# The first phase of a gated-scan and expert kernel: constants and small products to GpSimd, its products in halves, other step and store times

## The chip, the cores and the metric

One core of one Trainium2 chip runs the whole program. The metric is device time in microseconds (us) for one execution; lower is better. TensorE (PE) does matrix products and transposes, VectorE (DVE), ScalarE (ACT) and GpSimd (POOL) do elementwise work, and SyncE (SP) only issues transfers (DMA). Each engine runs its own instruction list in order. GpSimd also issues transfers, those whose rows are picked by a list of indices.

## What is computed

Two steps follow each other. First a gated recurrence runs along 4 sequences of 5056 positions with 256 features. Then each of the 20224 resulting rows is given to one of 8 experts, at most 2528 rows each, by going through all row-expert scores from the largest down; every expert is a two-layer network.

```python
f = lower_bound + (1 - lower_bound) * sigmoid(f_logit)
for t in range(S):
    h = f[:, t] * h + (1 - f[:, t]) * x[:, t]
    y[:, t] = h
...
logits = x @ w_gate
for idx in np.argsort(-logits.flatten()):
    tok, e = idx // E, idx % E
    if assigned[tok] >= 0 or counts[e] >= cap:
        continue
    assigned[tok] = e
...
out[mask] = np.maximum(x[mask] @ w1[e], 0) @ w2[e]
```

## The kernel before

The program has two phases. This document is about the first one, which I call the prelude: it takes about the first 159 us.

**The prelude's loop.** The rows are cut into 158 tiles of 128, and the loop `for i in range(NCH + 1)` takes them in 40 chunks of four tiles (the last has two). In pass `i`, SP issues the load of chunk `i+3` (`load`: one transfer for the gate logits, into tile `fl`, one for x, into tile `xl`; four buffers of each). `fwd(i)` transposes both on TensorE (into PSUM tiles `pf` and `pb`), ScalarE makes the gate `f` (tile `fg`) from `pf`, and VectorE runs the recurrence as two scans into tile `g`. `sig(i+2)` takes the sigmoid of a later chunk on ScalarE and then multiplies it into x on GpSimd, one instruction of 1024 columns. `back(i-1)` multiplies the scanned chunk by a matrix `iw` that turns it back and gives the 8 router scores (PSUM tile `pr`); VectorE and ScalarE copy `pr` into the row tile `hr`, GpSimd copies the scores into `X`, and SP stores `hr` to the scratch array `hbuf` in DRAM. There are 22 buffers for `hr`, so stores can lag; `SR = 0.5` and the line with `stored` say how far.

**What runs beside it.** `build(2)` emits two deferred VectorE instructions per pass that make constants. `prep(c0, c1)` finds the best expert of 32 tiles at a time, in five steps: a maximum (`M`), a comparison (`TMP`), a product with `kc` (on GpSimd up to tile 128, except the last piece before tile 72), another maximum (`A`), and a one-hot table (`O`). `early` picks one expert from the first 72 tiles, loads its weights by index (tile `r`), lists 896 of its rows (`g1` is a comparison of a ramp `IO` with an offset; `blocks` makes the row numbers `ids`), and `first_rows` gathers these rows from `hbuf`. `early` yields once per pass; each resumed piece goes to the head of a pass, ahead of `fwd(i)`'s scans on VectorE.

**The second phase** (`moe`) starts with transposes of the gathered rows (tile `pt`) and runs the experts while the rest of the assignment is worked out beside them. `Pace` keeps a count of expected engine times, by which small pieces of work are placed between matrix products; the order is fixed when the program is built.

In the profile nearly all instructions carry the line of one helper, L100, so they are told apart by the tiles that they write and read.

Of the kernel before, what the change touches and what calls it, by code (L numbers as in the profile page):

```python
# [106 lines left out]
def kernel(ctx: ExitStack, tc: tile.TileContext, x: bass.AP, f_logit: bass.AP,  # L107
# [9 lines left out]
    P = 128  # L117
# [27 lines left out]
    chunks = [(t0, min(KT, NT - t0), min(KT, NT - t0) * P // KT) for t0 in range(0, NT, KT)]  # L145
    NCH = len(chunks)
    RING = 22
    SR = 0.5
    PS, RW, CP = 2, NT - CE, 136
    LA = 4  # L150
    SPIN = (9, 4), (5, 2)

# [57 lines left out]
    late = []  # L210

    class Later:
        def __getattr__(self, op):
            return lambda *args, **kw: late.append((op, args, kw))
    lv = Later()

    def build(n):
        while late and n:
            op, args, kw = late.pop(0)
            getattr(nc.vector, op)(*args, **kw)  # L220
            n -= 1
    kc = consts.tile([P, E], F32, name="kc")
    lv.tensor_scalar(kc, IO[:, :E], -1.0, float(E), op0=OP.mult, op1=OP.add)


    IO8 = IO[:, :16].unsqueeze(2).to_broadcast([P, 16, 8])
    njt = []
    for st in (256.0, 16.0, 1.0):
        t = consts.tile([P, 16, 8], F32, name=f"njt{int(st)}")
        lv.tensor_scalar(t, IO8, st, None, op0=OP.mult)  # L230
        njt.append(t)
    thr0 = consts.tile([P, 16, 8], I16, name="thr0")
    lv.tensor_scalar(thr0, IO8, 4096.0, -32768.0, op0=OP.mult, op1=OP.add)
    tri = consts.tile([P, P], BF, name="tri")
    lv.tensor_scalar(tri, IO[:, :P], pv, None, op0=OP.is_gt)
    ones = consts.tile([P, P], F32, name="ones")
    lv.memset(ones, 1.0)
    onec = consts.tile([P, NX], F32, name="onec")
    lv.memset(onec, 1.0)
# [6 lines left out]
    lv.tensor_copy(fi, ii)  # L246
    bm = consts.tile([P, 8, E], F32, name="bm")
    lv.tensor_scalar(bm, IO[:, :8].unsqueeze(2).to_broadcast([P, 8, E]), fi[:, 1:2], None,
                            op0=OP.is_equal)

    selv = consts.tile([P, 16], F32, name="selv")
    lv.tensor_scalar(selv, IO[:, :16], fi[:, 2:3], None, op0=OP.is_equal)
# [8 lines left out]
    lv.tensor_scalar(j16, IO[:, :16].unsqueeze(2).to_broadcast([P, 16, E]), 1.0, None, op0=OP.add)  # L261

    at16 = consts.tile([P, 16, E], F32, name="at16")
    lv.tensor_copy(at16, IO[:, :16].unsqueeze(2).to_broadcast([P, 16, E]))
    lv.memset(at16[:, 0], 16.0)

    nsub = consts.tile([P, P], BF, name="nsub")
    prev = consts.tile([P, P], F32, name="prev")
    lv.tensor_scalar(prev, IO[:, :P], -1.0, pv, op0=OP.add, op1=OP.is_equal)
    lv.tensor_tensor(nsub, ident, prev, op=OP.subtract)  # L270
# [18 lines left out]
    wb = consts.tile([P, 3], F32, name="wb")  # L289
    wk = consts.tile([P, 3], F32, name="wk")  # L290
    for j, (m, o) in enumerate(((2 * P, 0), (2 * P, P), (P, 0))):
        lv.tensor_scalar(wb[:, j:j + 1], pv, float(E * m + o), None, op0=OP.add)
        lv.memset(wk[:, j:j + 1], float(-m))


    X = state.tile([P, NC, E], F32, name="X")
# [431 lines left out]
    def early(wi, ids):  # L728

        def sums(ps):  # L730
            for g in range(CE // 8):
                nc.tensor.matmul(ps[:, :64], ones_b, O[:, 8 * g:8 * g + 8].rearrange("p c e -> p (c e)"), start=(g == 0),
                                 stop=(g == CE // 8 - 1))
        yield sums
        ps = beside[0]
        v.tensor_reduce(SC8, ps[:, :64].rearrange("p (c e) -> p e c", e=E), AX.X, OP.add)
        v.tensor_scalar(Q8, SC8, float(EARLY), 1.0e6, op0=OP.is_lt, op1=OP.mult)
        v.tensor_tensor(Q8, Q8, SC8, op=OP.add)
        v.tensor_reduce(few, Q8, AX.X, OP.min)
        yield  # L740
        v.scalar_tensor_tensor(Q8, Q8, few, kc, op0=OP.is_equal, op1=OP.mult)
        v.tensor_reduce(ecode, Q8, AX.X, OP.max)
        v.scalar_tensor_tensor(wi, wk, ecode, wb, op0=OP.mult, op1=OP.add)
        first_weights(0)
        yield
        ranks(0, CE)
        first_weights(1)
        yield
        first_weights(2)
        w = CE + 2  # L750

# [12 lines left out]
        g1 = {}  # L764
        nb = EARLY // P
        for b0 in range(0, nb, 2):
            n = min(2, nb - b0)
            if b0 % 4 == 0:
                g1 = ohp.tile([P, 512], BF, name="g1")
                v.tensor_scalar(g1, IO, st[:, b0 // 4:b0 // 4 + 1], None, op0=OP.is_ge)  # L770
                yield

            def rows(ps):
                for b in range(n):
                    nc.tensor.matmul(ps[:, b * w:(b + 1) * w], g1[:, (b0 + b) % 4 * P:((b0 + b) % 4 + 1) * P],
                                     RAE[:, :w], start=(b == 0), stop=(b == n - 1), skip_group_check=True)
# [66 lines left out]
    def sig(i, which=None, between=lambda: None):  # L843
        np_ = chunks[i][2]
        if which is not False:
            for a, b in halves(0, i):
                nc.scalar.activation(FT[i][:np_, a:b], FT[i][:np_, a:b], AF.Sigmoid, scale=-1.0)
        if which is not True:
            for a, b in halves(1, i):
                mine = 1 < i < NCH - 1  # L850
                (nc.gpsimd if mine else nc.vector).tensor_mul(XT[i][:np_, a:b], FT[i][:np_, a:b], XT[i][:np_, a:b])
                if a == 0:
                    between()

# [11 lines left out]
    def fwd(i):  # L866
# [29 lines left out]
    def back(i, job=None):  # L896
        t0, n, _ = chunks[i]
        HR[i] = pring.tile([P, KT, ROW], F32, name="hr")
        for k in range(n):
# [43 lines left out]
    def prep_step(n):
        while preps and n:
            at = next(preps[0], None)
            if at is None:
                preps.pop(0)
            else:
                n = n - 1 if at == 'k' else 0
# [32 lines left out]
    for i in range(NCH + 1):  # L982
# [736 lines left out]
```

## Time and profile before

| what | value |
|---|---|
| median of three runs | 1148.47 us (1148.03 to 1148.62) |
| the profiled execution: time | 1148.47 us |
| its span, first to last instruction | 1146.7 us |
| TensorE busy over the span | 1129.9 us (99%) |
| TensorE busy in 100 to 150 us | 48.41 of 50 |
| TensorE busy in 250 to 300 us | 50.00 of 50 |
| first transpose of the second phase starts | 158.69 us |

The span lies 1.77 us below the time of the same execution. Times in the rows below count from the span's start. A row of a timeline gives the start, the duration, the engine, the operation with its tiles, and in square brackets how long the engine sat idle before it and what ended that. Neighbouring instructions of one kind are merged into a row with their count.

### The profile page before, as it was taken

What the parts mean: (1) busy time and instruction counts of PE and PEld (TensorE: products, weight loads), DVE (VectorE), ACT (ScalarE), POOL (GpSimd) and SP (SyncE); (2) the same over time, 40 slices, a digit from 0 to 9 for tenths busy, and PEclk for the clock granted to TensorE, in tenths of its full rate; (3) what the DMA queues carried; (4) which work ended last, traced back from release to release, by engine and by line L of the source; (5) the groups of instructions that cost most, each with busy time, mean ns of one, the idle gap of its engine ahead of it and who ended that gap; (6) DMA issues with size and microseconds to landing.
All of it is one profiled execution on the core that took longest, in us unless ns stands there. A gap on an engine that the chain in (4) does not pass through costs nothing.

```text
span 1146.7 us, 21286 instructions
## 1 busy us (share of the span) xinstructions
PE 1129.9 (99%) x7905; PEld 1008.9 (88%) x7905; DVE 764.8 (67%) x2233; ACT 542.1 (47%) x1141; POOL 477.6 (42%) x486
## 2 busy tenths in 40 slices
PE   9999989999999999999999999999999999999997
PEld 7999879989888888888889888898889888888887
DVE  7999997778777446776875877656444643463342
ACT  7889873263337532643544444345434532242221
POOL 5777642243335663333433433343334333433322
PEclk9999999999999999999999999999999999999999
DMA  9999995131131111311311311131113111321100
GB/s 353 374 355 371 394 341 152 38 112 43 48 111 39 40 52 50 115 48 42 120 47 43 112 47 41 48 115 48 46 43 110 58 42 49 108 62 46 42 32 32
DMA packets 52947, 125.23 MB, mean 109 GB/s; under 512 B 8563, under 2 KB 28789, under 8 KB 51685
## 3 DMA queue, kind: packets, MB, share of 16 engines
q0 software_dynamic: 20016, 61.01, 16.5%
q1 hardware_dynamic: 32544, 62.78, 15.5%
q8 instruction: 64, 1.05, 0.4%
q14 instruction: 47, 0.38, 0.1%
q10 hardware_dynamic: 276, 0.01, 0.0%
HBM read 81.79 MB, written 42.10 MB: 108 GB/s over the span
## 4 chain that ended last, share of the span: by engine, by line
PE 91%; DMA 3%; DVE 2%; issue 1%; ACT 1%; POOL 1%; POOLq 0%; DVEq 0%; ACTq 0%; SPq 0%
PE pw L100 39%; PE py L100 35%; PE rt L100 7%; PE pr L100 5%; PE pb L100 2%; PE pf L100 2%; DVE g L100 1%; PE pt L100 1%; DMA fl<-in_f_logit_dram 1%; DMA hbuf<-hr 1%; DMA r<-in_moe_w_dram,wi 1%; DVE hl L100 0%; ACT fg L100 0%; POOL out_dram L100 0%; ACT hh L100 0%
## 5 line engine op out<-in xcount | busy, mean ns | idle before, releaser
L100 PE MATMUL py<-w2s,hh 128*128 128x256 f32 (+2 forms) x2120 | 434.4, 296 | 0.0
L100 ACT ACTIVATE hh<-pw 128x512 fp32r<-128x512 f32 (+3 forms) x328 | 190.8, 582 | 496.9 <-PE pw L100 439.7
L100 DVE SCALAR_TENSOR_TENSOR hl<-pw,hh 128x512 fp32r<-128x512 f32 (+3 forms) x328 | 219.3, 669 | 214.4 <-ACT hh L100 213.1
L100 PEld LDWEIGHTS py<-w2s,hh 128*128 128x128 f32 (+1 forms) x2120 | 341.9, 188 | 20.8 <-issue 0.2
L100 PE MATMUL py<-w2s,hl 128*128 128x256 f32 x1136 | 319.8, 282 | 0.0
L100 POOL DMA_INDIRECT out_dram<-y,ids x160 | 162.7, 1017 | 304.7 <-ACT hh L100 248.2
L100 POOL DMA_INDIRECT fl<-hbuf,ids x160 | 164.4, 1028 | 267.6 <-ACT hh L100 193.6
L100 PE MATMUL pw<-xh,xl 128*128 128x512 f32 (+3 forms) x672 | 231.6, 387 | 1.2 <-DVE hl L100 0.9
L100 PEld LDWEIGHTS py<-w2s,hl 128*128 128x128 f32 x1136 | 212.8, 187 | 2.0
L100 PEld LDWEIGHTS pw<-xh,xl 128*128 128x128 f32 x672 | 124.8, 189 | 19.5 <-DVE hl L100 1.3
L100 PE MATMUL pw<-xl 128*128 128x512 f32 (+3 forms) x336 | 130.5, 389 | 0.1
L100 PE MATMUL pw<-xl,w1h 128*128 128x512 f32 (+1 forms) x320 | 127.0, 397 | 0.0
L100 PE MATMUL pw<-xh,w1h 128*128 128x512 f32 (+1 forms) x320 | 126.3, 395 | 0.0
L100 PE MATMUL pw<-xh,w1l 128*128 128x512 f32 (+1 forms) x320 | 126.2, 394 | 0.0
L100 POOL TENSOR_TENSOR xl<-fl,xl 128x1024 f32<-128x1024 f32 x37 | 87.7, 2369 | 40.2 <-ACT fl L100 22.0
L100 DVE TENSOR_TENSOR_SCAN g<-fg,g,pb 128x512 f32<-128x512 f32 (+4 forms) x78 | 92.8, 1227 | 6.8 <-ACT fg L100 6.1
L100 PE MATMUL pr<-iw,g 128*128 128x136 f32 x632 | 81.1, 280 | 0.5 <-ACT hr L100 0.5
L100 ACT ACTIVATE junk<-rt,r 128x182 bf16<-128x182 f32 (+2 forms) x153 | 61.4, 402 | 37.3 <-DVE r L100 32.7
L100 PEld LDWEIGHTS pr<-iw,g 128*128 128x128 f32 x632 | 76.4, 190 | 1.0 <-ACT hr L100 0.9
L100 PEld LDWEIGHTS pw<-xh,w1l 128*128 128x128 f32 x320 | 60.2, 188 | 11.3
L100 PEld LDWEIGHTS pw<-xl 128*128 128x128 f32 x336 | 63.7, 190 | 5.9 <-DVE xl L100 0.5
L100 PEld LDWEIGHTS pw<-xh,w1h 128*128 128x128 f32 x320 | 60.4, 189 | 8.0
(271 smaller groups left out, 1537.6 us busy)
## 6 DMA issues: line engine op xcount, KB each, us to landing
hbuf<-hr SPq DMA_DIRECT2D x39, 528.0 KB, 9.9
fl<-in_f_logit_dram SPq DMA_DIRECT2D x38, 512.0 KB, 6.7
xl<-in_x_dram SPq DMA_DIRECT2D x38, 512.0 KB, 7.2
fl<-hbuf,ids POOLq DMA_INDIRECT x160, 2.8
out_dram<-y,ids POOLq DMA_INDIRECT x160, 2.4
fl<-in_f_logit_dram SPq DMA_DIRECT2D x3, 256.0 KB, 4.1
xl<-in_x_dram SPq DMA_DIRECT2D x3, 256.0 KB, 4.5
r<-in_moe_w_dram,wi POOLq DMA_INDIRECT x27, 5.3
```

Source lines behind the costliest of these rows:

```text
L100: r = f(*args, **kw)
```

## The change

Eight edits, all in the prelude. Constants that VectorE made are made on GpSimd, partly ahead of the loop. The GpSimd product of each chunk is cut into two instructions of 512 columns (for chunk 2 the second half goes to VectorE). In `prep` the product with `kc` goes to GpSimd for all pieces up to tile 136, and two passes lie between it and the maximum that reads it; each pass runs one step. In `early` four small operations go to GpSimd and two of its steps come a pass later each. The comparison `g1` is written in the form that also adds up its result (into a column that nobody reads). `f` is made by a copy with a constant 1.0 instead of an identity with a column of ones. The third `hr` copy of even chunks below 18 goes from VectorE to ScalarE. Stores run at 0.6 of the passes up to the 18th, then pause, then go on one per pass from pass 35.

```diff
-    SR = 0.5
-    PS, RW, CP = 2, NT - CE, 136
+    SR = 0.6
+    RW, CP = NT - CE, 136
...
     kc = consts.tile([P, E], F32, name="kc")
-    lv.tensor_scalar(kc, IO[:, :E], -1.0, float(E), op0=OP.mult, op1=OP.add)
+    ramp(kc, [[-1, E]], E)
...
-    lv.tensor_scalar(tri, IO[:, :P], pv, None, op0=OP.is_gt)
+    lg_.tensor_scalar(tri, IO[:, :P], pv, None, op0=OP.is_gt)
...
-        v.tensor_scalar(Q8, SC8, float(EARLY), 1.0e6, op0=OP.is_lt, op1=OP.mult)
-        v.tensor_tensor(Q8, Q8, SC8, op=OP.add)
+        nc.gpsimd.tensor_scalar(Q8, SC8, float(EARLY), 1.0e6, op0=OP.is_lt, op1=OP.mult)
+        nc.gpsimd.tensor_tensor(Q8, Q8, SC8, op=OP.add)
+        yield
         v.tensor_reduce(few, Q8, AX.X, OP.min)
+        nc.gpsimd.tensor_scalar(Q8, Q8, few, None, op0=OP.is_equal)
+        nc.gpsimd.tensor_tensor(Q8, Q8, kc, op=OP.mult)
         yield
-        v.scalar_tensor_tensor(Q8, Q8, few, kc, op0=OP.is_equal, op1=OP.mult)
         v.tensor_reduce(ecode, Q8, AX.X, OP.max)
...
-                v.tensor_scalar(g1, IO, st[:, b0 // 4:b0 // 4 + 1], None, op0=OP.is_ge)
+                v.tensor_scalar(g1, IO, st[:, b0 // 4:b0 // 4 + 1], 0.0, op0=OP.is_ge, op1=OP.add, accum_out=esc[:, 6:7])
...
                 mine = 1 < i < NCH - 1
-                (nc.gpsimd if mine else nc.vector).tensor_mul(XT[i][:np_, a:b], FT[i][:np_, a:b], XT[i][:np_, a:b])
+                for c, e in ((a, (a + b) // 2), ((a + b) // 2, b)) if mine else ((a, b),):
+                    (nc.gpsimd if mine and (i > 2 or c == 0) else nc.vector).tensor_mul(XT[i][:np_, c:e], FT[i][:np_, c:e], XT[i][:np_, c:e])
...
-            nc.scalar.activation(f[:, h, :w], pf[h][:, :w], AF.Identity, scale=nomlb[:, h:h + 1], bias=one)
+            nc.scalar.activation(f[:, h, :w], pf[h][:, :w], AF.Copy, scale=nomlb[:, h:h + 1], bias=1.0)
...
-            if k == 0 or k == 2 and i % 2 == 0 and i < CE // KT:
+            if k == 0:
                 nc.vector.tensor_copy(HR[i][:, k], pr)
...
-        few_ = c1 == CE
-        far = nc.gpsimd if c1 <= 128 and not few_ else v
         v.tensor_reduce(m_, x_, AX.X, OP.max)
-        yield 'end' if few_ else 'k'
         v.tensor_tensor(t_, x_, bcl(m_, e - c0), op=OP.is_ge)
-        yield 'k'
-        far.tensor_tensor(t_, t_, bce(kc, e - c0), op=OP.mult)
-        yield 'k'
+        (nc.gpsimd if c1 <= CP else v).tensor_tensor(t_, t_, bce(kc, e - c0), op=OP.mult)
+        yield
+        yield
         v.tensor_reduce(a_, t_, AX.X, OP.max)
-        yield 'end' if few_ else 'k'
+        if not CE - 8 <= c1 <= CE:
+            yield
         v.tensor_tensor(O[:, c0:e], bce(kc, e - c0), bcl(a_, e - c0), op=OP.is_equal)
-        yield 'k'
+        yield
...
-        if i + 2 < NCH:
-            sig(i + 2)
+        for k in range(i + 2 - (i == 1), min(i + 3, NCH) if i else 0):
+            sig(k)
...
-            while stored < min(i - 1, int(SR * (i - 1)) + (i > 30)):
+            while stored < min(i - 1, max(min(int(SR * i), CE // KT), CE // KT + i - NCH + 6)):
                 store(TURN[stored])
                 stored += 1
-        if i >= 4:
-            build(2)
+        if i >= 2:
+            build(4)
...
-        prep_step(99 if i == NCH else 3 if done == CE and upto < CE + 8 else PS if done < CE else (i != NCH - 4) + (i > NCH - 3))
+        prep_step()
```

The first place is VectorE's list at the first `prep` piece (passes 9 to 12). A scan is printed there as SCALAR_TENSOR_TENSOR `g<-fg,g,pb`, two per pass. Before:

```order
L100 TENSOR_REDUCE M_171<-X 128x32
L100 TENSOR_TENSOR TMP<-X,M_171 128x256
L100 SCALAR_TENSOR_TENSOR g<-fg,g,pb 128x512 x2
L100 COPY hr<-pr 128x264
L100 TENSOR_SCALAR bm<-IO,fi 128x64
L100 TENSOR_SCALAR selv<-IO,fi 128x16
L100 TENSOR_REDUCE A_172<-TMP 128x32
L100 SCALAR_TENSOR_TENSOR g<-fg,g,pb 128x512 x2
```

The same place in the changed kernel:

```order
L100 TENSOR_REDUCE M_186<-X 128x32
L100 TENSOR_TENSOR TMP<-X,M_186 128x256
L100 SCALAR_TENSOR_TENSOR g<-fg,g,pb 128x512 x2
L100 COPY hr<-pr 128x264
L100 SCALAR_TENSOR_TENSOR g<-fg,g,pb 128x512 x2
L100 COPY hr<-pr 128x264
L100 TENSOR_REDUCE A_187<-TMP 128x32
L100 SCALAR_TENSOR_TENSOR g<-fg,g,pb 128x512 x2
```

The maximum `A`, which reads GpSimd's product, stood one pair of scans behind the comparison `TMP`, and now stands two pairs behind it; the constants `bm` and `selv` are gone from VectorE here.

The second place is VectorE's list at the second `g1` of `early`. Before, it stood alone between two pairs of scans, in pass 34:

```order
L100 COPY hr<-pr 128x264
L100 TENSOR_SCALAR g_2081<-IO,st 128x512
L100 SCALAR_TENSOR_TENSOR g<-fg,g,pb 128x512 x2
L100 COPY hr<-pr 128x264
```

In the changed kernel it comes in pass 36, in its summing form, behind the two first steps of the last `prep` piece:

```order
L100 COPY hr<-pr 128x264
L100 TENSOR_REDUCE M_186<-X 128x32
L100 TENSOR_TENSOR TMP<-X,M_186 128x256
L100 TENSOR_SCALAR g_2223,esc<-IO,st 128x512
L100 SCALAR_TENSOR_TENSOR g<-fg,g,pb 128x512 x2
```

Three instructions now share the place that one had.

The third place is SP's list at the end of the loads, up to the last one (64 rows). Before:

```order
L923 DMA hbuf<-hr 128x4x264 x2
L181 DMA fl<-in_f_logit_dram 128x1024
L181 DMA xl<-in_x_dram 128x1024
L181 DMA fl<-in_f_logit_dram 128x1024
L181 DMA xl<-in_x_dram 128x1024
L923 DMA hbuf<-hr 128x4x264
L181 DMA fl<-in_f_logit_dram 128x1024
L181 DMA xl<-in_x_dram 128x1024
L181 DMA fl<-in_f_logit_dram 128x1024
L181 DMA xl<-in_x_dram 128x1024
L923 DMA hbuf<-hr 128x4x264
L181 DMA fl<-in_f_logit_dram 64x1024
```

In the changed kernel:

```order
L931 DMA hbuf<-hr 128x4x264
L181 DMA fl<-in_f_logit_dram 128x1024
L181 DMA xl<-in_x_dram 128x1024
L181 DMA fl<-in_f_logit_dram 128x1024
L181 DMA xl<-in_x_dram 128x1024
L181 DMA fl<-in_f_logit_dram 128x1024
L181 DMA xl<-in_x_dram 128x1024
L181 DMA fl<-in_f_logit_dram 128x1024
L181 DMA xl<-in_x_dram 128x1024
L931 DMA hbuf<-hr 128x4x264
L181 DMA fl<-in_f_logit_dram 64x1024
```

Before, 18 stores stand ahead of the last load, four of them in its last stretch. Now 19 stand ahead of it, but 18 of these lie further up, and only one among the last four pairs of loads.

## Rows read from the trace of the kernel before

**Rows 1.** Chain of waits, 27 to 29 us (start, length, what).
```profile
27.00 1.85 PE pr L100 x16
28.86 0.87 PE pf L100 x8
```

**Rows 2.** Timeline, 48 to 55 us, three engines.
```profile
48.81 0.73 POOL L100 TENSOR_TENSOR TMP<-TMP,kc 128x256 f32<-128x256 f32 x1
...
49.57 0.42 DVE L100 TENSOR_REDUCE A<-TMP 128x32 f32<-128x256 f32 x1 [0.79 <-POOL TMP L100]
...
50.55 1.04 PE L100 MATMUL pf<-ident,fl 128*128 128x128 f32 x8
...
54.75 1.04 PE L100 MATMUL pf<-ident,fl 128*128 128x128 f32 x8
```

**Rows 3.** Timeline, 79 to 85 us, VectorE and TensorE.
```profile
79.16 0.42 DVE L100 TENSOR_REDUCE A<-TMP 128x32 f32<-128x256 f32 x1 [1.38 <-POOL TMP L100]
...
80.01 1.04 PE L100 MATMUL pf<-ident,fl 128*128 128x128 f32 x8
...
84.49 1.04 PE L100 MATMUL pf<-ident,fl 128*128 128x128 f32 x8
```

**Rows 4.** Timeline, 126 to 143 us, TensorE.
```profile
126.23 1.04 PE L100 MATMUL pf<-ident,fl 128*128 128x128 f32 x8
...
134.43 1.04 PE L100 MATMUL pf<-ident,fl 128*128 128x128 f32 x8
...
138.03 1.04 PE L100 MATMUL pf<-ident,fl 128*128 128x128 f32 x8
...
142.79 1.04 PE L100 MATMUL pf<-ident,fl 128*128 128x128 f32 x8
```

**Rows 5.** Timeline, 127 to 141 us, VectorE and GpSimd.
```profile
127.89 1.76 DVE L100 TENSOR_TENSOR O<-kc,A 128x256 bf16<-128x256 f32 x1
...
135.23 2.36 POOL L100 TENSOR_TENSOR xl<-fl,xl 128x1024 f32<-128x1024 f32 x1 [2.55 <-ACT hr L100]
...
135.76 2.12 DVE L100 TENSOR_SCALAR g<-IO,st 128x512 bf16<-128x512 f32 x1
...
137.54 0.41 POOL L100 COPY X<-hr 128x32 f32<-128x32 f32 x1
137.80 2.44 DVE L100 TENSOR_TENSOR_SCAN g<-fg,g,pb 128x512 f32<-128x512 f32 x2
...
140.16 0.40 DVE L100 COPY hr<-pr 128x264 f32<-128x264 f32 x1
```

**Rows 6.** Timeline, 103 to 105 us, GpSimd and VectorE.
```profile
103.09 2.38 POOL L100 TENSOR_TENSOR xl<-fl,xl 128x1024 f32<-128x1024 f32 x1
...
104.20 0.28 DVE L100 TENSOR_SCALAR_CACHE_REDUCE EM<-A,esc 128x72 f32<-128x72 f32 x1
```

**Rows 7.** Timeline, 117 to 123 us; then transfers in 112 to 142 us.
```profile
117.73 1.04 PE L100 MATMUL pf<-ident,fl 128*128 128x128 f32 x8
...
118.77 1.06 ACT L100 ACTIVATE fl<-fl 128x1024 f32<-128x1024 f32 x1 [2.56 <-DMA fl<-in_f_logit_dram]
...
122.27 1.04 PE L100 MATMUL pf<-ident,fl 128*128 128x128 f32 x8
...
DMA packets 4838, 11.89 MB, mean 396 GB/s; under 512 B 353, under 2 KB 2667, under 8 KB 4707
```

**Rows 8.** Timeline, 147 to 161 us: the gathers and the second phase's first transposes.
```profile
147.22 1.08 POOL L100 DMA_INDIRECT fl<-hbuf,ids  x1 [2.77 <-DMA hbuf<-hr]
...
158.69 0.38 PE L100 MATMUL pt<-identr,fl 128*128 128x128 f32 x2
160.09 0.28 PE L100 MATMUL pt<-identr,fl 128*128 128x128 f32 x1 [1.03 <-DMA fl<-hbuf,ids]
```

**Rows 9.** Window 160 to 170 us: busy time of PE, PEld, DVE, ACT, POOL; granted clock; DMA.
```profile
160.00:170.00 10.00, 8.38 (x30) 5.92 (x31) 8.50 (x16) 6.98 (x11) 0.77 (x3) 0.83 1.09 350
```

**Rows 10.** ScalarE groups, shapes kept apart, 20 to 150 us: busy, mean ns, idle before.
```profile
L100 ACT ACTIVATE fg<-pf,one,nomlb 128x512 f32<-128x512 f32 x68 | 49.3, 781 | 1.5
```

More of the change, by code (lines that the diff above doesn't have):

```diff
@@ L212, with __init__, ramp @@
     class Later:
+        def __init__(self, eng):
+            self.eng = eng
         def __getattr__(self, op):
-            return lambda *args, **kw: late.append((op, args, kw))
-    lv = Later()
+            return lambda *args, **kw: late.append((self.eng, op, args, kw))
+    lv, lg_ = Later(nc.vector), Later(nc.gpsimd)
     def build(n):
         while late and n:
-            op, args, kw = late.pop(0)
-            getattr(nc.vector, op)(*args, **kw)
+            eng, op, args, kw = late.pop(0)
+            getattr(eng, op)(*args, **kw)
             n -= 1
+    def ramp(t, pattern, base=0, channel=0):
+        nc.gpsimd.iota(t, pattern=pattern, base=base, channel_multiplier=channel, allow_small_or_imprecise_dtypes=True)
     kc = consts.tile([P, E], F32, name="kc")
-    lv.tensor_scalar(kc, IO[:, :E], -1.0, float(E), op0=OP.mult, op1=OP.add)
-    IO8 = IO[:, :16].unsqueeze(2).to_broadcast([P, 16, 8])
+    ramp(kc, [[-1, E]], E)
     njt = []
-    for st in (256.0, 16.0, 1.0):
-        t = consts.tile([P, 16, 8], F32, name=f"njt{int(st)}")
-        lv.tensor_scalar(t, IO8, st, None, op0=OP.mult)
+    for st in (256, 16, 1):
+        t = consts.tile([P, 16, 8], F32, name=f"njt{st}")
+        ramp(t, [[st, 16], [0, 8]])
         njt.append(t)
     thr0 = consts.tile([P, 16, 8], I16, name="thr0")
-    lv.tensor_scalar(thr0, IO8, 4096.0, -32768.0, op0=OP.mult, op1=OP.add)
     tri = consts.tile([P, P], BF, name="tri")
-    lv.tensor_scalar(tri, IO[:, :P], pv, None, op0=OP.is_gt)
+    lg_.tensor_scalar(tri, IO[:, :P], pv, None, op0=OP.is_gt)
     ones = consts.tile([P, P], F32, name="ones")
-    lv.memset(ones, 1.0)
+    nc.gpsimd.memset(ones, 1.0)
     onec = consts.tile([P, NX], F32, name="onec")
-    lv.memset(onec, 1.0)
+    nc.gpsimd.memset(onec, 1.0)
+    lg_.tensor_scalar(thr0, njt[0], 16.0, -32768.0, op0=OP.mult, op1=OP.add)
     ii = consts.tile([P, 3], I32, name="ii")
@@ L245 @@
     fi = consts.tile([P, 3], F32, name="fi")
-    lv.tensor_copy(fi, ii)
+    lg_.tensor_copy(fi, ii)
     bm = consts.tile([P, 8, E], F32, name="bm")
-    lv.tensor_scalar(bm, IO[:, :8].unsqueeze(2).to_broadcast([P, 8, E]), fi[:, 1:2], None,
+    lg_.tensor_scalar(bm, IO[:, :8].unsqueeze(2).to_broadcast([P, 8, E]), fi[:, 1:2], None,
                             op0=OP.is_equal)
     selv = consts.tile([P, 16], F32, name="selv")
-    lv.tensor_scalar(selv, IO[:, :16], fi[:, 2:3], None, op0=OP.is_equal)
+    lg_.tensor_scalar(selv, IO[:, :16], fi[:, 2:3], None, op0=OP.is_equal)
     tot = consts.tile([P, 16, 8], F32R, name="tot")
@@ L260 @@
     j16 = consts.tile([P, 16, E], F32, name="j16")
-    lv.tensor_scalar(j16, IO[:, :16].unsqueeze(2).to_broadcast([P, 16, E]), 1.0, None, op0=OP.add)
+    ramp(j16, [[1, 16], [0, E]], 1)
     at16 = consts.tile([P, 16, E], F32, name="at16")
-    lv.tensor_copy(at16, IO[:, :16].unsqueeze(2).to_broadcast([P, 16, E]))
-    lv.memset(at16[:, 0], 16.0)
+    ramp(at16, [[1, 16], [0, E]])
+    nc.gpsimd.memset(at16[:, 0], 16.0)
     nsub = consts.tile([P, P], BF, name="nsub")
     prev = consts.tile([P, P], F32, name="prev")
-    lv.tensor_scalar(prev, IO[:, :P], -1.0, pv, op0=OP.add, op1=OP.is_equal)
-    lv.tensor_tensor(nsub, ident, prev, op=OP.subtract)
+    lg_.tensor_scalar(prev, IO[:, :P], -1.0, pv, op0=OP.add, op1=OP.is_equal)
+    lg_.tensor_tensor(nsub, ident, prev, op=OP.subtract)
     sq = consts.tile([P, 21], F32, name="sq")
@@ L291 @@
     for j, (m, o) in enumerate(((2 * P, 0), (2 * P, P), (P, 0))):
-        lv.tensor_scalar(wb[:, j:j + 1], pv, float(E * m + o), None, op0=OP.add)
-        lv.memset(wk[:, j:j + 1], float(-m))
+        ramp(wb[:, j:j + 1], [[1, 1]], E * m + o, 1)
+        nc.gpsimd.memset(wk[:, j:j + 1], float(-m))
     X = state.tile([P, NC, E], F32, name="X")
@@ L927, in prep, with prep_step @@
         x_, t_, m_, a_ = X[:, c0:e], TMP[:, c0:e], M0[:, c0:e], A1[:, c0:e]
-        few_ = c1 == CE
-        far = nc.gpsimd if c1 <= 128 and not few_ else v
         v.tensor_reduce(m_, x_, AX.X, OP.max)
-        yield 'end' if few_ else 'k'
         v.tensor_tensor(t_, x_, bcl(m_, e - c0), op=OP.is_ge)
-        yield 'k'
-        far.tensor_tensor(t_, t_, bce(kc, e - c0), op=OP.mult)
-        yield 'k'
+        (nc.gpsimd if c1 <= CP else v).tensor_tensor(t_, t_, bce(kc, e - c0), op=OP.mult)
+        yield
+        yield
         v.tensor_reduce(a_, t_, AX.X, OP.max)
-        yield 'end' if few_ else 'k'
+        if not CE - 8 <= c1 <= CE:
+            yield
         v.tensor_tensor(O[:, c0:e], bce(kc, e - c0), bcl(a_, e - c0), op=OP.is_equal)
-        yield 'k'
+        yield
     preps = []
[L943 to L949, printed above, removed]
+    def prep_step():
+        if preps and next(preps[0], preps) is preps:
+            preps.pop(0)
+            prep_step()
     sig(0, True)
@@ L1025 @@
             done += 32
[L1026 removed]
+        prep_step()
         while lows and lows[0] == 0:
```

## The prediction

> **What bounds the kernel now.** I read the busy time by stretches first: after 250 us TensorE has no idle left, so the edits can pay only in the prelude and at the step into the second phase. Then the chain of waits for the prelude. In its undisturbed stretches it is TensorE alone: a pass is the back product of 1.85 us and two groups of transposes of 0.87 us each [rows 1], together 3.6 us. I call whatever a pass takes beyond 3.6 us a stall, and read it off the starts of successive `pf` groups in the timeline of TensorE; then I look in the timelines of the other engines for what was late there. Four kinds of stall appear.
>
> First, VectorE waits for GpSimd's product `TMP`. It sits idle 0.79 us before the maximum `A` at 49.57 us, and the pass there takes 54.75 - 50.55 = 4.20 us, a stall of 0.60 [rows 2]. The same wait at 79.16 us is 1.38 us, and the pass takes 84.49 - 80.01 = 4.48 us, a stall of 0.88 [rows 3].
>
> Second, single VectorE instructions last far too long while GpSimd multiplies. A comparison `g1` lasts 2.12 us, from 135.76 to 137.88, and GpSimd's 2.36 us product runs from 135.23 to 137.59; the table `O` lasts 1.76 us [rows 5]. The scans queue behind them. The two passes from 126.23 take 8.20 us (stall 1.00), the pass from 138.03 takes 4.76 us (stall 1.16) [rows 4]. An instruction that adds up its result ran in 0.28 us in the middle of such a product [rows 6], so not every form is held.
>
> Third, ScalarE waits 2.56 us for a load at 118.77 us, shortly after the first expert's weights were fetched, and the pass takes 122.27 - 117.73 = 4.54 us (stall 0.94); from there the transfers run at 396 GB/s [rows 7].
>
> Fourth, at the step into the second phase TensorE waits 1.03 us for a gathered tile. The first gather had held GpSimd's list for 2.77 us, until a store to `hbuf` had landed [rows 8].
>
> **The change, part by part.**
>
> *Two passes between product and maximum.* The order of VectorE's list now puts two pairs of scans between the comparison and the maximum. A pair takes 2.44 us [rows 5], the product 0.73 [rows 2], so the product is there long before. Both stalls of the first kind go: 0.60 + 0.88 = 1.5 us. What would be late next there is the comparison itself, if it meets a GpSimd product (next point).
>
> *Halves and the summing form.* VectorE's room in a pass is 3.60 - 2.44 (scans) - 0.40 (`hr` copy) = 0.76 us [rows 1, 5]. A delay of the scans by up to about 0.7 us more is absorbed: the scans end 2.44 us after their `pb` group, and the second half of the next `pb` group comes 1.85 + 0.87 + 0.44 = 3.16 us after it. GpSimd's price for 512 columns comes from its two sizes, 256 columns at 0.73 us and 1024 at 2.36 [rows 2, 5]: 2.12 ns a column and 0.19 us fixed, so 1.27 us a half, 2.54 a pair. A held instruction then waits at most 1.27 us where it waited up to 2.36, provided that VectorE gets in between the halves. The rows speak for that: GpSimd's small copy that was issued at 137.54, as its product ended, lasted until 137.95, past the end of the held `g1` at 137.88, so the held instruction went ahead [rows 5]. `g1` itself, in the summing form, should not be held at all. I price it at 0.7 us: 0.28 for 72 columns [rows 6] and 0.42 for 256 in a maximum [rows 2] make 0.76 ns a column, so 0.62 for 512, and a little for the sum's own read. Below it would be 0.62, above it 2.0 (held for a half after all).
>
> What stays: in pass 31 `O` and `g1` now stand together (0.4 + 0.7; I price `O`, `M` and `TMP`, all over 256 columns, like the 0.42 of the maximum), in pass 36 `M`, `TMP` and `g1` (0.4 + 0.4 + 0.7). Free of GpSimd they overrun the room of 0.76 by 0.3 and 0.7 us, which is absorbed. With one wait for a half each they overrun by 1.6 and 2.0: stalls 0.9 and 1.3. I take the middle, 1.1 together. Of the 2.16 us of the second kind, 1.0 comes back (bounds: 2.16 and 0).
>
> [...]
>
> *ScalarE.* The gate `f` is 781 ns a half [rows 10] and now has a constant for its column of ones; the third copy of nine chunks comes to ScalarE (about 0.4 us each). Neither is on the path: in the undisturbed passes TensorE stands alone in the chain [rows 1], and where ScalarE is late it waits for a load [rows 7]. I take 0 for both. If ScalarE had no room at all, the nine copies would cost up to 3.6 us. [...]
>
> *Constants.* Some thirty small VectorE instructions go. They lay in the room of passes without a stall, except the two ahead of the wait at 49.57 us, whose time that wait hid anyway: 0. On GpSimd they and the halves must fit into 3.6 us: 2.54 + 0.2 to 0.4 for the scores' copy [rows 5] leaves over 0.6 us.
>
> *Stores.* By pass 30 there are 18 stores where there were 14, so 4 x 0.54 = 2.2 MB move ahead; then none until pass 35. Per undisturbed pass the load is 1.05 MB, and stores at 0.6 add 0.32: 1.37 MB in 3.6 us are 381 GB/s, at 0.5 they were 366. The transfers have shown 396 GB/s when backed up [rows 7], so the higher rate still fits. The weights (2.1 MB) come two passes later and again back up the queue, so I expect a wait as in rows 7 once, between passes 30 and 34. After that, with loads alone at 291 GB/s, it drains, where before it stayed full to the end. Sum 0 (bounds: 0.9 gained, 2.2 lost).
>
> *The gathers.* The last of the 18 stores that they wait for is now out by pass 30 and not 35. The wait of 2.77 us goes, the product of chunk 38 and the other gathers behind it on GpSimd move up by the same, and they have to land 1.4 us sooner against TensorE to cost nothing. 1.03 us comes back. Against it VectorE has two more small steps in this place (the last `ids`, the last `A`), some 0.3 us. I take 0.7 (bounds 0 and 1.5). [...]
>
> *Sum.* 1.5 + 1.0 + 0.7 = 3.2 us. The profiled span of 1146.7 becomes 1143.5, and with the 1.77 us around it the time is 1145.3 us; the profiled execution had the median's time, so the same holds for the median.
>
> **Rivals.**
>
> *More comes back.* Held instructions miss the products (2.1), loads no longer wait (0.9), the step gives 1.5 and a third of the clock (0.6): with 1.5 that is 6.6, 1141.9 us. For it: the pause of the stores. Against it: two places of VectorE's list got fuller.
>
> *The transfers take it back.* The earlier stores leave no slack, so every stall that goes returns as a wait for a load, and only the step pays, 0.7: 1147.8 us. For it: 396 GB/s against 381 asked. Against it: before the weights no load was late after the start, and after pass 30 the demand falls.
>
> *The halves don't do what they should*: both stand issued, and VectorE gets its turn only behind the second, so that the second kind stays at 2.16 or grows to 2.5 with the fuller places. The sum is 1.5 - 0.3 + 0.7 = 1.9: 1146.6 us. Against it stands the copy that was passed. [...]
>
> *GpSimd becomes the bound (slower).* If a half, with the waits that VectorE's own instructions put on it, takes over (3.60 - 0.25) / 2 = 1.67 us (0.25 for the scores' copy), every pass grows by the excess. From 1.8 us a half on, 0.26 us in 36 passes, 9.4 us, stand against the 3.2: 1154.7 us. From 1.72 us a half on it eats the gain (0.1 us in 36 passes), from 1.75 it is slower by more than 0.2%. Rows 2 and 5 say 1.27; against it stands only that no half of this shape has been seen.
>
> **Numbers.** A difference under 0.2% (2.3 us) can't be told from none. Forecast (gain 2.3 to 5) 0.53, more 0.13, transfers 0.14, halves 0.13, GpSimd 0.07. Faster by over 0.2%: 0.53 + 0.13 + a third of the halves = 0.70. Within: 0.14 + the rest = 0.23. Slower 0.07. The range goes from 1141.9 (the larger gain) to 1147.5, most of the way to the transfers' case; GpSimd and about a tenth beside it stay outside.
>
> **What would show it.** No wait of VectorE for `TMP`; `pf` to `pf` 3.6 us from 20 to 110 us. Halves near 1.27 us, `g1` near 0.7 wherever it falls. One late load between 118 and 130 us, none after. No wait of GpSimd for a store, and the first transpose of the second phase at 155 to 157 us instead of 158.69. I would be wrong if loads are late before 100 us, if held VectorE instructions last two halves, or if passes settle above 3.6 us with GpSimd without idle.

## The result, and the profile after

The changed kernel takes 1166.01 us (median of four runs, 1165.1 to 1167.08), the kernel before 1148.55 (1148.03 to 1149.36): a ratio of 1.0145, 95% interval 1.0133 to 1.0157. It is slower by 17.5 us, where I had forecast 3.2 us faster. The profiled execution took 1166.71 us with a span of 1164.8.

Read by stretches, the loss has one place. Windows of the changed kernel (stretch; busy us of PE, PEld, DVE, ACT, POOL with their instructions; granted clock; share of the DMA engines; GB/s):

```profile
150.00:160.00 10.00, 8.93 (x81) 8.13 (x78) 9.72 (x26) 8.43 (x17) 6.43 (x9) 1.00 1.08 357
160.00:170.00 10.00, 4.36 (x17) 2.95 (x17) 5.39 (x10) 1.93 (x2) 0.00 (x0) 0.95 1.09 343
170.00:180.00 10.00, 0.00 (x0) 0.00 (x0) 0.00 (x0) 0.00 (x0) 0.00 (x0) 0.50 0.97 302
180.00:190.00 10.00, 5.53 (x20) 4.90 (x21) 6.46 (x15) 4.24 (x8) 0.00 (x0) 0.53 0.01 4
190.00:200.00 10.00, 10.00 (x89) 8.69 (x88) 6.72 (x22) 3.23 (x10) 0.00 (x0) 1.00 0.01 2
```

For the whole of 170 to 180 us no engine computes; only the transfers run, at 302 GB/s, and TensorE's granted clock falls to 0.50; it is 0.53 in the next 10 us, and 1.00 in 190 to 200 us. Who waits for whom stands in the timeline of 158 to 190 us:

```profile
165.17 0.33 DVE L100 TENSOR_REDUCE A<-TMP 128x22 f32<-128x176 f32 x1
182.06 1.15 ACT L100 ACTIVATE w2s<-r 128x512 fp32r<-128x512 f32 x2 [20.13 <-DMA hbuf<-hr]
182.72 0.69 DVE L100 TENSOR_TENSOR w2s<-r,w2s 128x512 fp32r<-128x512 f32 x1 [17.23 <-ACT w2s L100]
183.12 0.58 ACT L100 ACTIVATE hh<-pw 128x512 fp32r<-128x512 f32 x1
...
184.47 0.80 PE L100 MATMUL pw<-xh,xl 128*128 128x512 f32 x1 [19.59 <-DVE hl L100]
...
187.20 0.63 PE L100 MATMUL py<-w2s,hh 128*128 128x256 f32 x2
```

Read it backwards. TensorE waits for `hl`, `hl` for ScalarE's `hh`, and `hh` stands behind `w2s` in ScalarE's list. `w2s` is the first expert's second weight matrix, converted from the fetched tile `r`. It waits 20.13 us, and not for its input: it waits for stores `hr` to `hbuf`. In the kernel before, the same `w2s` ran at 164.10 us with no idle before it; the first `pw` product, this `w2s` and the first `py` stand there so:

```profile
161.53 0.61 PE L100 MATMUL pw<-xh,xl 128*128 128x512 f32 x1 [0.34 <-ACT xh L100]
...
164.10 1.15 ACT L100 ACTIVATE w2s<-r 128x512 fp32r<-128x512 f32 x2
...
170.18 0.39 PE L100 MATMUL py<-w2s,hh 128*128 128x256 f32 x2
```

The changed kernel's chain of waits names the last of the stores:

```profile
173.13 8.82 DMA hbuf<-hr
```

It landed at 173.13 + 8.82 = 181.95 us, and `w2s` started at 182.06.

Why a weight tile waits for a store of rows is told by the addresses in the built program. The 22 buffers of `hr` lie from byte 115744 of SBUF on, 4224 bytes each. The second phase's pools are laid over them when the prelude's pools close. `w2s` (pool `wa2`, 16384 bytes from 149664) covers buffers 8 to 11 in both kernels, and may be written once the last rows held there are stored. Which rows these are is not fixed: a new `hr` tile takes the buffer that was released, so the order of the stores decides the order in which buffers come round. Before, buffers 8 to 11 last held chunks 18, 20, 21 and 19, which stand in the list `TURN` (the order of the stores) ahead of some 17 others. With the new rule they last held chunks 38, 39, 19 and 21, and 38 and 39 are the last stores of all.

The rows that answer to [rows 2 to 8, 10], in the changed kernel:

```profile
51.90 0.41 DVE L100 TENSOR_REDUCE A<-TMP 128x32 f32<-128x256 f32 x1
...
110.53 1.40 DVE L100 TENSOR_TENSOR TMP<-X,M 128x256 f32<-128x256 f32 x1
...
122.56 0.73 DVE L100 TENSOR_SCALAR_CACHE_REDUCE g<-IO,st 128x512 bf16<-128x512 f32 x1
...
126.26 1.06 ACT L100 ACTIVATE fl<-fl 128x1024 f32<-128x1024 f32 x1 [2.92 <-DMA fl<-in_f_logit_dram]
...
144.90 1.08 POOL L100 DMA_INDIRECT fl<-hbuf,ids  x1
...
157.96 0.54 PE L100 MATMUL pt<-identr,fl 128*128 128x128 f32 x4
...
159.19 0.49 PE L100 MATMUL pw<-xh,xl 128*128 128x512 f32 x1 [0.35 <-ACT xh L100]
```

Groups of instructions, ScalarE in 20 to 150 us and GpSimd in 10 to 158 us (busy, mean ns):

```profile
L100 ACT ACTIVATE fg<-pf,nomlb 128x512 f32<-128x512 f32 x69 | 43.7, 686 | 1.6
...
L100 POOL TENSOR_TENSOR xl<-fl,xl 128x512 f32<-128x512 f32 x73 | 92.0, 1281 | 31.3 <-ACT fl L100 21.8 <-ACT hr L100 5.6 <-PE pr L100 3.6
```

The prelude itself is faster: the wait for `TMP` is gone, the half product of GpSimd lasts 1281 ns, `g1` 0.73 us, the first gather waits for no store, and the first `pw` product starts at 159.19 us where it was 161.53. Then 2.3 us of gain meet a wait of 20 us.

### The profile page after: what moved, and what is told of

Read it like the earlier page. It is cut to its first block, busy times and chain, and to the rows that moved or that the text cites. A ratio compares the mean times of both kernels' runs of the same rounds, so it can differ in the third digit from the quotient of the medians.

```text
span 1164.8 us, 21352 instructions
## 1 busy us (share of the span) xinstructions
PE 1130.2 (97%) x7905; PEld 1009.9 (87%) x7905; DVE 758.3 (65%) x2200; ACT 541.7 (47%) x1150; POOL 487.9 (42%) x550
## 4 chain that ended last, share of the span: by engine, by line
PE 89%; DMA 3%; issue 2%; DVE 2%; POOL 1%; ACT 1%; SPq 1%; POOLq 0%; DVEq 0%; ACTq 0%
PE pw L100 38%; PE py L100 34%; PE rt L100 7%; PE pr L100 4%; PE pb L100 2%; PE pf L100 2%; DMA fl<-in_f_logit_dram 2%; PE pt L100 1%; SPq L931 1%; DVE g L100 1%; DMA hbuf<-hr 1%; DMA r<-in_moe_w_dram,wi 1%; POOL xl L100 1%; ACT hh L100 0%; POOL out_dram L100 0%
## 5 line engine op out<-in xcount | busy, mean ns | idle before, releaser
L100 POOL TENSOR_TENSOR xl<-fl,xl 128x512 f32<-128x512 f32 x73 | 92.0, 1281 | 31.3 <-ACT fl L100 21.8
```

What stands on the lines that cost most here:

```text
L100: r = f(*args, **kw)
```

## The experiments

Theory A is the one above: the order of the stores decides which chunk lies under `w2s`. Rival B says that the backlog of stores makes the wait wherever the buffers lie, rival C that the work moved to GpSimd and VectorE delays the conversion. The runs were made on more than one chip: the kernel before took 1159.12 us beside the first four runs, on one chip, and 1149.34 and 1150.29 beside the next four and the last three, both on another. So each ratio is to the kernel before as it ran beside them on the same chip, and places in the prelude are compared by their distance from the `pf` group of chunk 2; kernels with one run are judged by such places, except where the difference is over 15 us.

| kernel | `pf` of chunk 2 | first `pw` | `w2s` starts (its wait) | first `py` | time | kernel before there | ratio |
|---|---|---|---|---|---|---|---|
| before | 14.23 | 161.53 | 164.10 (none) | 170.18 | 1148.55 | | |
| after | 14.62 | 159.19 | 182.06 (20.1) | 187.20 | 1166.01 | 1148.55 | 1.0145 |
| e1 | 15.00 | 162.72 | 165.35 (none) | 172.90 | 1159.22 | 1159.12 | 1.0004 [0.9984, 1.0023] |
| e2 | 14.57 | 162.21 | 181.85 (16.9) | 186.99 | 1175.76 | 1159.12 | 1.0132 [1.0099, 1.0165] |
| e3 | 14.78 | 160.01 | 162.65 (none) | 169.12 | 1155.75 | 1159.12 | 0.9967 [0.9951, 0.9983] |
| e4 | 14.30 | 161.57 | 184.48 (20.2) | 189.62 | 1177.13 | 1159.12 | 1.0153 [1.0123, 1.0184] |
| e5 | 14.57 | 161.43 | 164.00 (none) | 170.38 | 1150.12, one run | 1149.34 | |
| e6 | 15.10 | 162.15 | 164.75 (none) | 170.67 | 1151.0, one run | 1149.34 | |
| e7 | 15.02 | 161.66 | 164.29 (none) | 170.28 | 1150.15, one run | 1149.34 | |
| e8 | 14.62 | 158.08 | 160.70 (none) | 167.80 | 1146.38 | 1149.34 | 0.9970 [0.9959, 0.9982] |
| e9 | 14.45 | 158.31 | 160.96 (none) | 167.39 | 1147.02 | 1150.29 | 0.9975 [0.9964, 0.9987] |
| e10 | 14.45 | 159.80 | 184.41 (21.9) | 189.55 | 1168.86, one run | 1150.29 | |
| e11 | 14.78 | 158.03 | 181.12 (20.4) | 186.26 | 1166.01, one run | 1150.29 | |

**e1, the changed kernel with the old store rule.**

```diff
-    SR = 0.6
+    SR = 0.5
...
-            while stored < min(i - 1, max(min(int(SR * i), CE // KT), CE // KT + i - NCH + 6)):
+            while stored < min(i - 1, int(SR * (i - 1)) + (i > 30)):
```

> The changed kernel with the old rule for the stores alone (0.5 a pass, one pass later); all else as changed. In the changed kernel ScalarE's first expert conversion (w2s) waits 20.1 us for the last stores, because with the new rule the buffers of the ring that the pool wa2 is laid over (numbers 8 to 11) last held chunks 38, 39, 19, 21; with the old rule they last held 18, 20, 21, 19, which are stored first. Theory A (the store rule decides which chunk lies under the second phase's buffers): no wait of w2s above 2 us, the first pw matmul at 158 to 161 us, time 1142 to 1147 us. Rival B (the backlog of stores on the DMA engines makes the wait, wherever the buffers lie): also fast, 1142 to 1148. Rival C (the products in halves and the steps moved to GpSimd make the conversion or its input late, the stores only end there): the wait stays, 1160 us or more.

**e2, the kernel before with the new store rule alone.**

```diff
-    SR = 0.5
+    SR = 0.6
...
-            while stored < min(i - 1, int(SR * (i - 1)) + (i > 30)):
+            while stored < min(i - 1, max(min(int(SR * i), CE // KT), CE // KT + i - NCH + 6)):
```

> The kernel before with the new rule for the stores alone (0.6 a pass, started a pass earlier, all 39th-and-later stores late); prelude arithmetic as before. Theory A: buffers 8 to 11 last hold chunks 38, 39, 19, 21, so w2s waits 15 to 20 us for the last store and the time is 1164 to 1170 us, 15.5 to 21 above before: the rule alone makes the loss. Rival B: the same, 1164 to 1170. Rival C: no long wait, 1146 to 1150 us.

**e3, the changed kernel with three pools opened in another order.**

```diff
+    wb_ = pool("wb", 1)
+    wa2 = pool("wa2", 1)
     yp = pool("yp", YB)
-    wa2 = pool("wa2", 1)
-    wb_ = pool("wb", 1)
```

> The changed kernel, with the three second-phase pools wb, wa2, yp opened in the order wb, wa2, yp where it was yp, wa2, wb. So w2s lies at 158112 instead of 149664, over buffers 10 to 13, which last held chunks 19, 21, 20, 18, all stored early; the new stores and the whole prelude stay. Theory A: the long wait is gone, first pw at 157 to 160 us, time 1142 to 1147 us. Rival B: the backlog of stores is the same, so the wait stays above 10 us and the time above 1158 us. Rival C: the same as B.

**e4, the kernel before with the same three lines reordered.**

> The kernel before, with the same three pools reordered and nothing else: its stores and prelude stay. Here buffers 10 to 13 last held chunks 21, 19, 39, 37, so w2s now lies over the last chunks' buffers. Theory A: w2s waits 15 to 20 us for the stores of chunks 39 and 37, time 1163 to 1170 us, a loss made without any part of the change. Rivals B and C: nothing of the stores or of the prelude changed, so 1147 to 1150 us.

The four ran together. In e1 and e3 `w2s` starts with no idle before it; in e2 and e4 it waits, as the timelines of ScalarE show, in the order e1, e3, e2, e4:

```profile
165.35 1.14 ACT L100 ACTIVATE w2s<-r 128x512 fp32r<-128x512 f32 x2
```

```profile
162.65 1.15 ACT L100 ACTIVATE w2s<-r 128x512 fp32r<-128x512 f32 x2
```

```profile
181.85 1.15 ACT L100 ACTIVATE w2s<-r 128x512 fp32r<-128x512 f32 x2 [16.90 <-DMA hbuf<-hr]
```

```profile
184.48 1.15 ACT L100 ACTIVATE w2s<-r 128x512 fp32r<-128x512 f32 x2 [20.16 <-DMA hbuf<-hr]
```

My ranges in us were worked out from 1148.5 us, so all four times lie 6 to 12 us above them. Taken as ratios, e3 and e4 lie inside theory A's ranges and e2 just under its own (1.0132, expected from 1.0135 on); e1 misses: I had expected a gain, and its first `pw` at 158 to 161 us, and it has neither (1.0004, 162.72). Rival C falls with e2 and e4, where no arithmetic of the prelude differs from before. Rival B falls with e3, where the stores are those of the changed kernel and the wait is gone, and with e4, where the stores are those of before and the wait is there. e4 makes a loss as large as the change's (1.0153) with three lines that no edit of the change touched.

e1 shows a second thing. Its wait is gone, yet it gains nothing: the first gather again waits, GpSimd being idle 2.25 us ahead of it (timeline of GpSimd):

```profile
147.95 1.08 POOL L100 DMA_INDIRECT fl<-hbuf,ids  x1 [2.25 <-PE pr L100]
```

Its release is put down to `pr`, but it starts 132.95 us behind the `pf` group of chunk 2, in the changed kernel, which differs in the stores alone, 130.28 us behind it. GpSimd's product for chunk 38 stands behind this gather, and e1's chain of waits goes on from there: its second half at 150.28 us, then TensorE's `pb` at 151.62.

**e5, the kernel before with the new `prep` and `prep_step` alone** (the lines between product and maximum).

```diff
...
-        yield 'k'
-        far.tensor_tensor(t_, t_, bce(kc, e - c0), op=OP.mult)
-        yield 'k'
+        (nc.gpsimd if c1 <= CP else v).tensor_tensor(t_, t_, bce(kc, e - c0), op=OP.mult)
+        yield
+        yield
         v.tensor_reduce(a_, t_, AX.X, OP.max)
...
```

> The kernel before with the new order of the table's steps alone (two passes between GpSimd's product TMP and the maximum A, the product on GpSimd up to chunk 136, at most one step a pass). Theory (first term of the sum, 1.5 us): VectorE no longer waits for TMP, the passes that began at 50.55 and 80.01 us before take 3.6 us and not 4.20 and 4.48, the pf group that stood at 91.69 us stands 1.4 to 1.6 us sooner. Rival: a comparison TMP<-X,M or a table O meets a product of GpSimd more often now, is held for 1 us or more, and less than 0.8 us comes back.

VectorE's maxima, from its timeline, with no idle before them:

```profile
52.65 0.41 DVE L100 TENSOR_REDUCE A<-TMP 128x32 f32<-128x256 f32 x1
...
80.53 0.41 DVE L100 TENSOR_REDUCE A<-TMP 128x32 f32<-128x256 f32 x1
```

The `pf` groups behind them start 3.61 and 3.60 us apart (50.83 to 54.44 and 79.67 to 83.27), and the group that stood at 91.69 stands at 90.47. Measured from chunk 2 that is 75.90 us instead of 77.46: 1.56 us sooner, so 1.5 was right. At the first `pw` only 0.44 of it is left (146.86 us from chunk 2 instead of 147.30). Two things take the rest. The four passes from 132.22 to 149.01 us take 16.79 us, where they took 15.68: `g1` is held much as before (1.98 us at 138.12), and now the comparison `TMP` is held too (1.11 at 143.14; before 0.40 at 152.08), so late in the prelude the rival was right in part. And the first gather again stands behind 2.21 us of idle.

**e6, the kernel before with halves alone.**

```diff
-                (nc.gpsimd if mine else nc.vector).tensor_mul(XT[i][:np_, a:b], FT[i][:np_, a:b], XT[i][:np_, a:b])
+                for c, e in ((a, (a + b) // 2), ((a + b) // 2, b)) if mine else ((a, b),):
+                    (nc.gpsimd if mine else nc.vector).tensor_mul(XT[i][:np_, c:e], FT[i][:np_, c:e], XT[i][:np_, c:e])
```

> The kernel before with GpSimd's products in two halves alone (two of 512 columns for one of 1024); g1 stays in the old form. Theory (second term): VectorE gets in between the halves, so no VectorE instruction is held for more than about 1.3 us: g1 of 512 columns lasts at most 1.4 us where it was 2.12, O at most 1.4 where it was 1.76; the two passes from 126.23 and the one from 138.03 us lose 1.1 us together and not 2.16. Rival: both halves stand issued and VectorE gets in only behind the second: held instructions of 1.8 to 2.4 us remain.

**e7, the kernel before with the summing form of `g1` alone.**

```diff
-                v.tensor_scalar(g1, IO, st[:, b0 // 4:b0 // 4 + 1], None, op0=OP.is_ge)
+                v.tensor_scalar(g1, IO, st[:, b0 // 4:b0 // 4 + 1], 0.0, op0=OP.is_ge, op1=OP.add, accum_out=esc[:, 6:7])
```

> The kernel before with the four g1 comparisons in the summing form alone; GpSimd's products stay whole. Theory: the form alone frees them: each g1 lasts 0.65 to 0.75 us even where a product of 2.36 us runs beside it, and the pass that took 4.76 us from 138.03 takes 3.6 to 3.9. Rival: the form is held as well (1.3 us or more beside a product), and what made it 0.73 in the changed kernel was the halves or a place without a product.

Only two of the four comparisons named there lie in the prelude, and the edited line makes those two alone. Rows of the two timelines, VectorE and GpSimd; first e6, then e7:

```profile
115.03 2.69 POOL L100 TENSOR_TENSOR xl<-fl,xl 128x512 f32<-128x512 f32 x2 [0.28 <-ACT fl L100]
116.51 1.50 DVE L100 TENSOR_SCALAR g<-IO,st 128x512 bf16<-128x512 f32 x1
...
135.96 0.48 DVE L100 TENSOR_SCALAR g<-IO,st 128x512 bf16<-128x512 f32 x1
136.42 2.52 POOL L100 TENSOR_TENSOR xl<-fl,xl 128x512 f32<-128x512 f32 x2 [2.63 <-ACT hr L100]
```

```profile
135.36 2.38 POOL L100 TENSOR_TENSOR xl<-fl,xl 128x1024 f32<-128x1024 f32 x1 [2.55 <-ACT hr L100]
135.89 0.74 DVE L100 TENSOR_SCALAR_CACHE_REDUCE g<-IO,st 128x512 bf16<-128x512 f32 x1
```

e7 is clear: in the place of the 2.12 us of [rows 5], wholly inside a whole product, the summing form takes 0.74 us. The pass that took 4.76 us takes 3.75 (138.15 to 141.90), as expected. e6 is weaker: the old form takes 0.48 us where no product runs (there it happened to miss one), and 1.50 where it is issued as a second half begins, so held for about one half (e6's last 1284 ns on average) and no more. That is a little over my bound of 1.4 and under the rival's 1.8. Its three passes lose 0.56 us together, less than the 1.1 expected, but the passes ahead of them have cost e6 0.61 us more than in the kernel before (112.61 us from chunk 2 to the group at 127.71, before 112.00). At the first `pw` e6 keeps 0.25 us of its gain and e7 0.66.

**e8, e3 with two constants a pass and the first choice's small steps as before.**

```diff
-            build(4)
+            build(2)
...
-        nc.gpsimd.tensor_scalar(Q8, SC8, float(EARLY), 1.0e6, op0=OP.is_lt, op1=OP.mult)
-        nc.gpsimd.tensor_tensor(Q8, Q8, SC8, op=OP.add)
-        yield
+        v.tensor_scalar(Q8, SC8, float(EARLY), 1.0e6, op0=OP.is_lt, op1=OP.mult)
+        v.tensor_tensor(Q8, Q8, SC8, op=OP.add)
         v.tensor_reduce(few, Q8, AX.X, OP.min)
-        nc.gpsimd.tensor_scalar(Q8, Q8, few, None, op0=OP.is_equal)
-        nc.gpsimd.tensor_tensor(Q8, Q8, kc, op=OP.mult)
         yield
+        v.scalar_tensor_tensor(Q8, Q8, few, kc, op0=OP.is_equal, op1=OP.mult)
```

> The changed kernel with w2s moved as in the third run, two constants a pass instead of four, and the first choice's small steps as they were before (on VectorE, a pass sooner). Theory (two stalls that the change itself made): sq and the casts behind it no longer stand together beside a product, so the pass of 4.0 us near 33 us takes 3.6 and the sum of stalls to 37 us falls by 0.8 to 0.9; the ranks no longer stand in the pass of a held comparison, so the pass of 4.9 us from 112.8 us takes 3.6 to 4.2. If the loads don't take it back, the first pw stands at 157.5 to 159 us (160.0 in the third run, 159.2 in the changed kernel), and the ratio to before is 0.994 to 0.997. Rival: the loads, already late by 2.8 us at 126 us, take it back: the waits of ScalarE for fl grow by what was won, first pw at 159 to 160.5, ratio 0.996 to 0.999.

The two stalls are told by rows of the changed kernel's timeline: a constant of 21 columns held for a half of GpSimd's product, with more constants behind it and ahead of the scans.

```profile
29.34 2.51 POOL L100 TENSOR_TENSOR xl<-fl,xl 128x512 f32<-128x512 f32 x2
...
30.65 1.25 DVE L100 TENSOR_SCALAR sq<-sq 128x21 f32<-128x21 f32 x1
31.81 0.27 DVE L100 CAST RS<-pv 128x1 bf16<-128x1 f32 x3
```

In the changed kernel the two passes from 29.06 us take 7.77 us, in e8 7.20: 0.57 back, less than the 0.8 to 0.9 expected. The two passes from 109.23 take 8.55 us, in e8 (from 108.66) 8.10: 0.45 back, not 0.7 to 1.3, since a held `TMP` (0.98 us at 111.02) and one overfull pass stay. First `pw` at 158.08 us, inside the 157.5 to 159 of the theory; 0.9970 also stands at its bound. The loads took little: ScalarE waits for `fl` 6.0 us in all between 100 and 140 us, 5.7 in the changed kernel.

**e9, e10, e11: e8 with the store rate at 0.65, 0.55 and 0.7** (e9 shown).

```diff
-    SR = 0.6
+    SR = 0.65
```

> The eighth kernel (w2s moved, constants spread, first choice as before) with stores at 0.65 a pass instead of 0.6; the stores that the gathers need are out about two passes sooner. Theory A: w2s now lies over chunks 18, 19, 21, 20, all stored early: no long wait; the pause of the stores before the weights is longer, so the late loads after 116 us cost 0.5 to 1.5 us less than in the eighth run (1.5 us in the passes from 124 to 133); ratio to before 0.995 to 0.998. Rival (the transfers are full at 0.65 and loads are late before 100 us): 0.998 to 1.001.

> The eighth kernel with stores at 0.55 a pass, nearer to the rate before. The ring's buffers come round in another order: w2s (over buffers 10 to 13) now lies over chunks 21, 20, 18 and 38, so theory A asks for a wait of 13 to 20 us for the store of chunk 38 and a time 14 to 20 us above before, although the rate is milder than in the eighth run, which has no such wait. Rival (a rate or a backlog that is too high makes the wait): 0.55 lies between 0.5 and 0.6, both without it in a fitting layout, so no long wait and the time of before less 1 to 4 us.

> The eighth kernel with stores at 0.7 a pass: w2s lies over chunks 39, 18, 20 and 21, so theory A asks for a wait of 15 to 20 us for the last store and 15 to 20 us above before, where 0.65, with chunks 18, 19, 21, 20 in the same place, has none. Rival (the backlog alone): the last stores are out sooner at the higher rate, so no wait, or a shorter one than at 0.55.

`w2s` in e9, from the timeline of ScalarE:

```profile
160.96 1.16 ACT L100 ACTIVATE w2s<-r 128x512 fp32r<-128x512 f32 x2
```

The waits of ScalarE in 100 to 200 us, first e10, then e11 (engine and tile, waited for: us in total, times, longest):

```profile
ACT w2s L100 <- DMA hbuf<-hr: 21.9, 1, 21.9
```

```profile
ACT w2s L100 <- DMA hbuf<-hr: 20.4, 1, 20.4
```

At 0.6 and 0.65 there is no such wait, at 0.55 and 0.7 there is, each time as the chunk under `w2s` says (the waits are somewhat longer than the 13 to 20 and 15 to 20 us expected; the times lie 18.6 and 15.7 us above before, one run each). No rate and no backlog does that; rival B is out a second time. e9 itself is no better than e8 within the intervals: the expected 0.5 to 1.5 us from fewer late loads didn't come, its longest wait of ScalarE for `fl` is 3.53 us, in e8 1.8.

## Why the prediction was wrong

**The step that failed is "Stores ... Sum 0 (bounds: 0.9 gained, 2.2 lost)".** It asked what earlier stores do to the transfers and to the gathers, and left out a third reader: the tile that is next laid over the buffers. It needed a term for the new order in which buffers come free, and that term is some 20 us: `w2s` waited 20.13 us, and without this wait (e3) the ratio is 0.9967 and not 1.0145. Net of what the prelude had won, `w2s` started 17.96 us later (182.06 instead of 164.10), and the first `py` 17.02 us later, although the first `pw` had been 2.34 us sooner. From the first `py` to the end the two kernels take 976.5 and 977.6 us; 17.0 + 1.1 = 18.1, which is the difference of the spans. The prediction even says that the transfers stayed full to the end before; it asked of late stores only what they do to loads and gathers. In the kernel before no engine sits idle for a store between 150 and 200 us, although the backlog is as long there, and e4 shows why: the last chunks lay elsewhere.

**Two passes, 1.5 us: right** (1.56 in e5; no wait for `TMP` in the changed kernel).

**Halves and summing form: priced right, worth less than 1.0 where it counts.** The half took 1281 ns (1270 priced) and `g1` 0.73 (0.7). The pass of 1.16 us of stall was won whole in the changed kernel (138.22 to 141.82 us: 3.60). But the five passes ahead of it lose 2.44 us (117.78 to 138.22 us, against 18.0) where they lost 2.30 before: late loads (2.92 us at 126.26 alone) took the place of the held `O` (0.58 us now, at 122.05). I had expected one late load; ScalarE waited for one five times between 100 and 140 us, three times before. So the rival "the transfers take it back" was partly true.

**Constants, 0: wrong by 0.57 us**, shown by e8. The step looked at the constants that leave VectorE and not at those that stay (`sq`, the casts); four at once in one pass, one of them held for 1.25 us, overran its room.

**First choice (`early`'s pick of an expert): left out.** Moved a pass later, its rank steps met a held `TMP` (1.40 us): the pass from 112.83 us took 4.95 us. e8 returned 0.45 of that.

**ScalarE, 0: not contradicted**; the gate fell from 781 to 686 ns a half, by 95.

**The gathers, 0.7: right in kind, and hidden in the sum.** e1 and e3 ran on one chip and differ in the stores and in the place of `w2s`; the first `pw` stands 147.72 us from chunk 2 in the one (162.72 - 15.00) and 145.23 in the other. So the early stores are worth some 2.5 us at this step once the rest is faster, and e5, e6 and e7 show the other side: under the old stores 0.25 to 0.66 us of their gains is left there. Their first gather starts 132.69, 133.15 and 131.96 us from chunk 2, much as in the kernel before (132.99), though the passes that they stand in start 1.73, 0.99 and 1.68 us sooner than there. In e2, with the new stores and the old arithmetic, the first gather starts at 129.87 us and TensorE waits for no gathered tile, but the first `pw` is no sooner either (147.64 against 147.30). There the work of the last chunks is late: TensorE sits idle 1.02 us before `pb` at 155.41 us, and 0.72 and 0.93 us until ScalarE's `hr` copies free the way for `pr` at 157.40 and 159.98; what delayed that work is not separated. So the terms did not add up one by one: neither the first three nor the last gained much alone. No run shows the 0.6 us of clock that the rival "More comes back" counts: over 160 to 200 us the granted clock was 0.96 in the kernel before, 0.95 in e1 and 1.00 in e3, and from the first `pw` to the first `py` they took 8.65, 10.18 and 9.11 us, so what the clock alone is worth there is not separated.

Without the wait the sum comes out right: e3 measures 0.9967 [0.9951, 0.9983], and 1145.3 / 1148.47 is 0.9972. Part of that is chance, since a stall that the sum had left out (first choice) and one priced too low (constants) stand against a step that gave more than 0.7.

## What to carry to other kernels

Where tiles come from a ring whose buffers are given out as they come free, and a later pool reuses its memory, the order of releases is part of the layout: after any change to when buffers are released, list which tile each buffer held last and which later tile is laid over it. A late transfer is harmless only if nobody waits for its buffer, so ask this of every store that lags, not only of its readers. The three lines of e3 turned 1.0145 into 0.9967, and e8 (0.9970, on another chip than e3) has its first `pw` at 158.08 us, sooner than both kernels.

## What the runs showed of the hardware

TensorE was slow for some time after the stall: it did nothing from 164.89 to 184.47 us, its granted clock was 0.50 in 170 to 180 us and 0.53 in 180 to 190, and the first `py` pair took 0.63 us after it, 0.39 in the kernel before. An instruction of VectorE far smaller than GpSimd's product was held about as long as a larger one: in the changed kernel `sq`, 21 columns, took 1.25 us beside a half, and the comparison `TMP`, 256 columns, 1.40 (at 110.53 us). In the kernel before, `sq` took 0.18 us, where it stood between two products:

```profile
63.95 0.18 DVE L100 TENSOR_SCALAR sq<-sq 128x21 f32<-128x21 f32 x1
```

And the same kernel before differed by 10 us between two chips (1149.34 and 1159.12), so a gain of 3 us can be read only from runs on one chip or from places in the trace.
